# A feed-forward block in float32: both products by one step of a seven-product scheme, with the second weight matrix streamed from DRAM

## The chip, the cores and the metric

The kernel runs on one core of one Trainium2 chip. A core has TensorE (PE in the profile: matmuls; its weight loads are listed apart as PEld), VectorE (DVE), ScalarE (ACT), GpSimd (POOL), SyncE (SP, which here only issues DMAs) and 16 DMA engines. Tiles lie in SBUF, 128 partitions wide; matmul results go to PSUM, eight banks of 512 float32 values per partition. Each engine works through its own instructions in order and waits on semaphores for the others. The metric is the time of one execution on the device in microseconds (us), the median of several runs.

## The reference

Linear attention with a normalization, then a feed-forward block with squared ReLU. All arrays are float32, except that the two weight matrices arrive as float64.

```python
kv = np.einsum('bhsd,bhse->bhde', k, v)           # B=8, H=8, S=576, D=64
out = np.einsum('bhsd,bhde->bhse', q, kv)
rms = np.sqrt(np.mean(out * out, axis=-1, keepdims=True) + 1e-06)
x = out / rms * g_norm                            # then (B, H, S, D) -> (4608, 512)
h = x @ w_in                                      # 512 x 2048
r = np.maximum(h, 0.0)
y = (r * r) @ w_out                               # 2048 x 512
```

The two feed-forward products have 2 x 4608 x 512 x 2048 multiply-adds; the attention has far fewer.

## The kernel before

The 4608 tokens are worked off in nine strips of 512 (N_STRIP, four tiles of 128 tokens each). For each strip the attention must deliver `xt[s]`, the transposed features (128 partitions x 4 chunks of the model width x 512 tokens).

**Attention slices.** The attention is cut into small functions put into one list, `slices`: `transposed_query` and `key_value` for each of four pairs of heads of a batch, then `query` (four matmuls, square on ScalarE L226, reduction and Newton steps on VectorE L228 to L237, the scaled `x_n` L239) and `features` (four transposes L250, a scaled copy to `xt` on ScalarE L251). `key_value` also starts the loads of a later unit (`load_next`: ten DMAs on SP). `ready[s]` is the number of slices after which strip s has its features. `attend(n)` emits slices up to number n.

**Feed-forward.** `up(s, fc)` makes one chunk of 128 of the 2048 hidden features for the 512 tokens: four matmuls (K in four chunks) of 128 x 128 weights with 512 moving columns (L290), ReLU on ScalarE (L294), square on VectorE (L296). 16 such chunks stay in SBUF as `gt`. `down(s, i, part)` makes 128 tokens x 512 outputs: 16 matmuls in four parts (L307), then a copy to SBUF and a store. Results of both share four PSUM banks (`fpsum`).

**Order of the work.** The order is written out by hand (manual schedule): for each strip 16 `up` steps, then 16 `down` steps, and after every step `attend` emits the share of the next strip's slices that is due: by step i, (i + 1) / 29 of them. So the attention of strip s+1 lies between the matmuls of strip s.

**Weights.** Both matrices are to lie in SBUF as float32 for the whole run. They come as float64 words, and 32 pieces (16 of W_in, 16 of W_out, each 128 x 512 values, 512 KB) are converted by `convert`: two ScalarE operations (L142, L158), and on VectorE two TENSOR_SCALARs (L143, L148), a SCALAR_TENSOR_TENSOR (L153) and an integer add (L159). Three raw buffers; a piece's conversion issues the load of the piece three further on (L124). The conversions start before strip 0 and go on between its steps, three pieces for two steps, so that a piece of W_out is converted by the time `down` of strip 0 needs it.

Of the kernel before, what the change touches and what calls it, by code (L numbers as in the profile page):

```python
# [19 lines left out]
def kernel(  # L20
# [32 lines left out]
    N_TILE = n_tok // P  # L53
    NT = 4
    STRIP = NT * P
    N_STRIP = N_TILE // NT
# [3 lines left out]
    qkv_pool = ctx.enter_context(tc.tile_pool(name="qkv", bufs=3))  # L60
# [6 lines left out]
    raw_pool = ctx.enter_context(tc.tile_pool(name="raw", bufs=3))  # L67
    wtmp = ctx.enter_context(tc.tile_pool(name="wtmp", bufs=2))
    r_pool = ctx.enter_context(tc.tile_pool(name="r", bufs=2))
    g_pool = ctx.enter_context(tc.tile_pool(name="g", bufs=FC + 2))  # L70
    osb_pool = ctx.enter_context(tc.tile_pool(name="osb", bufs=2))
    apsum = ctx.enter_context(tc.tile_pool(name="apsum", bufs=4, space=bass.MemoryType.PSUM))
    fpsum = ctx.enter_context(tc.tile_pool(name="fpsum", bufs=4, space=bass.MemoryType.PSUM))
    ctx.enter_context(tc.manual_schedule())


# [25 lines left out]
    def load_next():  # L102
        u = next(to_load, None)
        if u is not None:
            load(*u)

    for _ in range(3):
# [6 lines left out]
    w_in_v = moe_w_in.rearrange("(kc p) (j f) -> j kc p f", p=P, f=WN)  # L114
    w_out_v = moe_w_out.rearrange("(fc p) e -> fc p e", p=P)
    pieces = [(w_in_v[j, kc], w_in[:, kc, ts(j, WN)]) for j in range(d_ff // WN) for kc in range(NP)]
    N_IN = len(pieces)
    pieces += [(w_out_v[fc], w_out[:, fc, :]) for fc in range(FC)]
    raw = []

    def load_piece():
        if len(raw) < len(pieces):
            t = raw_pool.tile([P, WN], I64, name="raw", tag="raw")
            nc.sync.dma_start(out=t, in_=pieces[len(raw)][0])  # L124
            raw.append(t)


    LEAST, MOST = 2.0**-15, float.fromhex("0x1.DFFFFEp+16")
    piece_at = [0]

    def convert(n):
        while piece_at[0] < min(n, len(pieces)):
            i = piece_at[0]
            words = raw[i].bitcast(I32).rearrange("p (n two) -> p n two", two=2)
            low = raw[i].bitcast(U32).rearrange("p (n two) -> p n two", two=2)[:, :, 0]
            high = words[:, :, 1]
            high_f = raw[i].bitcast(FP32).rearrange("p (n two) -> p n two", two=2)[:, :, 1]
            dest = pieces[i][1].bitcast(I32)


            c = wtmp.tile([P, WN], FP32, name="w_c", tag="w_c")
            nc.scalar.activation(c, high_f, AF.Abs)  # L142
            nc.vector.tensor_scalar(  # L143
                out=c, in0=c, scalar1=LEAST, scalar2=MOST, op0=ALU.max, op1=ALU.min
            )

            ci = c.bitcast(I32)
            nc.vector.tensor_scalar(  # L148
                out=ci, in0=ci, scalar1=3, scalar2=0x3FFFFFFF,
                op0=ALU.logical_shift_left, op1=ALU.bitwise_and,  # L150
            )

            nc.vector.scalar_tensor_tensor(  # L153
                out=dest, in0=high, scalar=-(2**30), in1=ci, op0=ALU.bitwise_and, op1=ALU.bitwise_or
            )

            r = wtmp.tile([P, WN], I32, name="w_r", tag="w_r")
            nc.scalar.activation(r, low, AF.Copy, scale=2.0**-29)  # L158
            nc.vector.tensor_tensor(out=dest, in0=dest, in1=r, op=ALU.add)  # L159
            load_piece()  # L160
            piece_at[0] += 1

    for _ in range(3):
        load_piece()
# [10 lines left out]
    qT, kvd, x_n, xt = {}, {}, {}, {}  # L175
# [67 lines left out]
    def features(n):  # L243
        s, i = divmod(n, NT)
        t = x_n.pop(n)
        if s not in xt:
            xt[s] = xt_pool.tile([P, NP, STRIP], FP32, name="xT", tag="xT")
        ps = apsum.tile([P, NP, P], FP32, name="xt_ps", tag="at")
        for p in range(NP):
            nc.tensor.transpose(ps[:, p, :], t[:, ts(p, P)], ident)  # L250
        nc.scalar.activation(xt[s][:, :, ts(i, P)], ps, AF.Copy, scale=g_col)  # L251

    slices, ready = [], {}
    for b in range(B):
        for p in range(NP):
            slices += [(transposed_query, (b, p)), (key_value, (b, p))]
        first = b // 2 * PAIR + (C if b % 2 else 0)
        ns = list(range(first, first + C + b % 2))
        for i, n in enumerate(ns + [None]):
            if n is not None:  # L260
                slices.append((query, (n,)))
            if i > 0:
                slices.append((features, (ns[i - 1],)))
                if ns[i - 1] % NT == NT - 1:
                    ready[ns[i - 1] // NT] = len(slices)
# [19 lines left out]
    gt = {}  # L285

    def up(s, fc):
        ps = fpsum.tile([P, STRIP], FP32, name="h_ps", tag="f")
        for kc in range(NP):
            nc.tensor.matmul(  # L290
                ps, lhsT=w_in[:, kc, ts(fc, P)], rhs=xt[s][:, kc, :], start=(kc == 0), stop=(kc == NP - 1)
            )
        r = r_pool.tile([P, STRIP], FP32, name="r", tag="r")
        nc.scalar.activation(r, ps, AF.Relu)  # L294
        t = g_pool.tile([P, STRIP], FP32, name="gt", tag="gt")
        nc.vector.tensor_tensor(out=t, in0=r, in1=r, op=ALU.mult)  # L296
        gt[fc] = t

    OQ = 4
    o_ps = [None]  # L300

    def down(s, i, part):
        if part == 0:
            o_ps[0] = fpsum.tile([P, d_model], FP32, name="o_ps", tag="f")
        n = FC // OQ
        for fc in range(part * n, (part + 1) * n):
            nc.tensor.matmul(  # L307
                o_ps[0], lhsT=gt[fc][:, ts(i, P)], rhs=w_out[:, fc, :], start=(fc == 0), stop=(fc == FC - 1)
            )
        if part == OQ - 1:  # L310
            o_sb = osb_pool.tile([P, d_model], FP32, name="o_sb", tag="o_sb")
            (nc.scalar.copy if i % 2 else nc.vector.tensor_copy)(o_sb, o_ps[0])  # L312
            for part_, rows in out_rows(NT * s + i):
                nc.sync.dma_start(out=rows, in_=o_sb[part_])

    for i in range(ready[0]):
        attend(i + 1)
        convert(i // 2 - 5)
    for s in range(N_STRIP):
        attend(ready[s])  # L320
        steps = [(up, (s, fc)) for fc in range(FC)]
        steps += [(down, (s, i, part)) for i in range(NT) for part in range(OQ)]
        goal = ready.get(s + 1, len(slices))
        for i, (fn, a) in enumerate(steps):
            if s == 0:

                convert(NP + 2 + 3 * i // 2)
            fn(*a)
            attend(ready[s] + (goal - ready[s]) * (i + 1) // (len(steps) - 3))


# [28 lines left out]
```

## Time and profile before

| | before |
|---|---|
| median of 3 runs | 1158.25 us (1158.03 to 1159.32) |
| the profiled execution, its own time | 1158.05 us |
| its span in the trace | 1156.2 us |
| granted TensorE clock, mean | 0.988 |
| TensorE busy | 1115.7 us (96%) |
| VectorE, ScalarE, GpSimd busy | 272.4, 210.7, 10.5 us |
| moved by DMA | 55.10 MB, 48 GB/s on average |

How to read the lines that follow. A line of the groups has: source line, engine, operation, output tile <- input tiles, shapes, count | busy us, mean ns of one instruction | idle us of its engine just before them and what ended it. The mean of a matmul is its latency from first to last element, with its way through the array; neighbours overlap, so the time that each adds is read from the distance between starts, or from the chain. A line of the chain of waits in order of time has: start, us, what was on the path, and of how many instructions. A line of the timeline has: start, us, engine, line, operation. A line of the windows has: window, its length, busy us and count of each engine, TensorE clock, share of the DMA engines, GB/s. A line of the DMA issues has: count, KB each, median us from issue to landing.

### The profile page before, as it was taken

To read this page: it belongs to the slowest core of one execution; us is meant where nothing else is said; L and a number is where in the kernel's file an instruction comes from. 1 tells how busy PE (TensorE), PEld (TensorE's weight loads), DVE (VectorE), ACT (ScalarE), POOL (GpSimd) and SP (SyncE) were. 2 spreads that over 40 slices of the span, in tenths; PEclk is the share of its full clock that TensorE was granted. 3 is DMA by queue.
4 is the path that set the end of the run, shared out by engine and by line. 5 is a ranking of instruction groups with operands and counts; after the bars stand their busy time and mean duration, and the time that the engine had idled before them with its cause. 6 is when DMAs were issued, how large, how long until landed. Compare 5 with 4: busy or idle time off the path is not lost.

```text
span 1156.2 us, 8506 instructions
## 1 busy us (share of the span) xinstructions
PE 1115.7 (96%) x3232; PEld 545.0 (47%) x3232; DVE 272.4 (24%) x590; ACT 210.7 (18%) x400; POOL 10.5 (1%) x70
## 2 busy tenths in 40 slices
PE   3699799999999999999999999999999999999998
PEld 3355354545445554454445444445445544444443
DVE  0789711212122122102111122102220122101200
ACT  1565311211121012101121112101220112001100
POOL 1000000000000000000000000000000000000000
PEclk8899899999999999999999999999999999999999
DMA  7567400220012100220012100230010000000000
GB/s 197 160 212 233 128 10 18 54 63 26 19 31 61 40 19 9 62 71 19 9 31 62 49 19 1 54 85 21 0 31 10 18 10 1 9 19 9 1 18 19
DMA packets 100169, 55.10 MB, mean 48 GB/s; under 512 B 83232, under 2 KB 91424, under 8 KB 100128
## 3 DMA queue, kind: packets, MB, share of 16 engines
q1 hardware_dynamic: 99968, 54.55, 17.0%
q8 instruction: 26, 0.43, 0.2%
q14 instruction: 15, 0.12, 0.0%
q10 hardware_dynamic: 160, 0.00, 0.0%
HBM read 45.09 MB, written 9.44 MB: 47 GB/s over the span
## 4 chain that ended last, share of the span: by engine, by line
PE 93%; SPq 2%; DVE 2%; DMA 1%; ACT 1%; issue 0%; DVEq 0%; ACTq 0%
PE h_ps L290 43%; PE o_ps L307 42%; PE kv_ps L197 2%; PE x_ps L223 2%; PE xt_ps L250 1%; PE t_ps L182 1%; SPq L91 1%; PE kv_ps L198 1%; SPq L95 1%; DMA raw<-in_moe_w_out_dram 0%; DMA q<-in_q_dram 0%; PE x_ps L218 0%; DVE w_c L148 0%; SPq L86 0%; DVE w_out L153 0%
## 5 line engine op out<-in xcount | busy, mean ns | idle before, releaser
L307 PE MATMUL o_ps<-w_out,gt 128*128 128x512 f32 x1152 | 513.0, 598 | 6.7 <-DVE w_out L159 6.7
L290 PE MATMUL h_ps<-xT,w_in 128*128 128x512 f32 x1152 | 508.3, 596 | 1.5 <-ACT xT L251 0.8
L290 PEld LDWEIGHTS h_ps<-xT,w_in 128*128 128x128 f32 x1152 | 215.4, 191 | 255.4 <-issue 248.2
L307 PEld LDWEIGHTS o_ps<-w_out,gt 128*128 128x128 f32 x1152 | 214.5, 191 | 255.4 <-issue 243.5
L296 DVE TENSOR_TENSOR gt<-r 128x512 f32<-128x512 f32 x144 | 99.6, 691 | 414.1 <-ACT r L294 414.1
L294 ACT ACTIVATE r<-h_ps 128x512 f32<-128x512 f32 x144 | 85.8, 596 | 365.5 <-PE h_ps L290 365.4
L228 DVE TENSOR_REDUCE ms<-sq 128x8 f32<-128x512 f32 x36 | 24.6, 684 | 157.3 <-ACT sq L226 157.3
L226 ACT ACTIVATE sq<-x_ps 128x512 f32<-128x512 f32 x36 | 21.4, 596 | 163.8 <-PE x_ps L223 140.1
L312 DVE COPY o_sb<-o_ps 128x512 f32<-128x512 f32 x18 | 12.5, 692 | 163.5 <-PE o_ps L307 163.4
L197 PEld LDWEIGHTS kv_ps<-v,k 128*128 128x128 f32 x256 | 35.9, 205 | 13.4 <-issue 13.4
L251 ACT ACTIVATE xT<-xt_ps,g_col 128x512 f32<-128x512 f32 x36 | 24.6, 683 | 93.2 <-PE xt_ps L250 93.2
L223 PEld LDWEIGHTS x_ps<-kvd,qT 128*128 128x128 f32 x256 | 33.6, 194 | 13.6 <-issue 13.6
L182 PE MATMUL t_ps<-ident,q 128*128 128x128 f32 x128 | 20.7, 288 | 18.6 <-DMA q<-in_q_dram 18.6
L197 PE MATMUL kv_ps<-v,k 128*128 128x128 f32 x256 | 36.3, 289 | 0.0
L223 PE MATMUL x_ps<-kvd,qT 128*128 128x128 f32 x256 | 34.1, 277 | 0.0
L312 ACT COPY o_sb<-o_ps 128x512 f32<-128x512 f32 x18 | 10.5, 586 | 123.8 <-PE o_ps L307 123.8
L182 PEld LDWEIGHTS t_ps<-ident,q 128*128 128x128 f32 x128 | 16.6, 148 | 33.9 <-issue 31.4
L250 PE MATMUL xt_ps<-ident,x_n 128*128 128x128 f32 x144 | 22.2, 278 | 9.7 <-DVE x_n L239 5.2
L250 PEld LDWEIGHTS xt_ps<-ident,x_n 128*128 128x128 f32 x144 | 18.0, 143 | 27.3 <-issue 16.2
L184 ACT COPY qT<-t_ps 128x512 f32<-128x512 f32 x32 | 18.6, 582 | 61.8 <-PE t_ps L182 61.8
L206 DVE COPY kvd<-kv_ps 64x64 f32<-64x64 f32 x32 | 7.3, 228 | 83.4 <-ACT kvd L205 83.2
L142 ACT ACTIVATE w_c<-raw 128x512 f32<-128x512 f32 x32 | 21.7, 678 | 28.3 <-DMA raw<-in_moe_w_out_dram 16.2
(32 smaller groups left out, 222.4 us busy)
## 6 DMA issues: line engine op xcount, KB each, us to landing
k<-in_k_dram SPq DMA_DIRECT2D x64, 128.0 KB, 3.0
v<-in_v_dram SPq DMA_DIRECT2D x32, 256.0 KB, 3.2
q<-in_q_dram SPq DMA_DIRECT2D x64, 128.0 KB, 3.0
raw<-in_moe_w_in_dram SPq DMA_DIRECT2D x16, 512.0 KB, 3.6
raw<-in_moe_w_out_dram SPq DMA_DIRECT2D x16, 512.0 KB, 3.7
out_dram<-o_sb SPq DMA_DIRECT2D x32, 256.0 KB, 2.3
k_rest<-in_k_dram SPq DMA_DIRECT2D x32, 32.0 KB, 2.9
v_rest<-in_v_dram SPq DMA_DIRECT2D x32, 32.0 KB, 2.7
```

The costliest lines, as they stand in the source:

```text
L142: nc.scalar.activation(c, high_f, AF.Abs)
L182: nc.tensor.transpose(ps[:, c, :], flat(t[:, c]), ident)
L197: nc.tensor.matmul(ps, lhsT=flat(tk[:, c]), rhs=tv[:, :, c, :], start=(c == 0), stop=False)
L223: nc.tensor.matmul(o, lhsT=qT[b, p][:, c_b, :], rhs=kvd[b, p], start=True, stop=True)
L228: nc.vector.reduce_sum(out=ms, in_=by_head(sq), axis=AX.X)
L250: nc.tensor.transpose(ps[:, p, :], t[:, ts(p, P)], ident)
L251: nc.scalar.activation(xt[s][:, :, ts(i, P)], ps, AF.Copy, scale=g_col)
L290: nc.tensor.matmul(ps, lhsT=w_in[:, kc, ts(fc, P)], rhs=xt[s][:, kc, :], start=(kc == 0), stop=(kc == NP - 1))
L294: nc.scalar.activation(r, ps, AF.Relu)
L296: nc.vector.tensor_tensor(out=t, in0=r, in1=r, op=ALU.mult)
L307: nc.tensor.matmul(o_ps[0], lhsT=gt[fc][:, ts(i, P)], rhs=w_out[:, fc, :], start=(fc == 0), stop=(fc == FC - 1))
L312: (nc.scalar.copy if i % 2 else nc.vector.tensor_copy)(o_sb, o_ps[0])
```

## The change

Both matrix products of a strip are done as 2 x 2 blocks by one step of Strassen's scheme in Winograd's form: seven block products instead of eight, with sums of blocks ahead of and behind them.

- **Blocks of `up`.** W_in is halved along the model width (KH = 2 chunks of 128) and along the hidden features (FH = 1024); the strip's features are halved along the model width and along the tokens (TH = 256). So a matmul in `up` now has 256 moving columns. `w_in` holds seven blocks: the four (one of them overwritten by a difference) and three sums.
- **Blocks of `down`.** The hidden values G are halved along the hidden features and the tokens, W_out along the hidden features and the outputs (DH = 256). Matmuls have 256 moving columns too.
- **Weights.** Pieces are the same size, but each has two runs of 256 columns. After four pieces of W_in, or two of W_out, GpSimd makes four sums or differences of 512 elements a partition (`sums_in`, `sums_out`). W_out's seven blocks don't stay in SBUF: after each two pieces they are written to a DRAM tensor of 7 MB (896 KB a time), and `stream` reads one block of 1 MB for each product of each `down`, three ahead, on SP. The pools of raw pieces and temporaries are closed after the conversions; the stream's three buffers and the output buffers take their space.
- **Order of conversions.** There are 44 items now (32 pieces, 12 groups of sums). Five are issued in each of the four groups of `up` of strip 0, a group ahead; what is left is issued in one block before `down` of strip 0.
- **Features.** `sums_x`, a new attention slice, makes four sums of the features on VectorE (512 elements each) once a strip's features are there.
- **Products.** A step `up(s, g, p)` is one block product for two feature chunks: 8 matmuls of 256 columns, into one bank. The order of products is 1, 2, 6, 5, 7, 3, 4. Products 6, 7 and 4 go on adding to the bank of product 1 (A), product 3 to that of product 5 (B); product 2 has bank C. In between, `combine` takes snapshots on ScalarE (after 1, 6 and 5) or adds bank and snapshot on VectorE (after 2, 7 and 3); product 4's bank is C21 itself. Bank A has two buffers, B and C one each.
- **After `up`.** ReLU and square are now a VectorE add out of PSUM and one VectorE instruction for three quarters, and two ScalarE instructions for the last. VectorE also makes G's sums: two in `up`, two long ones (2048 elements a partition) in `down`.
- **`down(s, p, i)`** is 8 matmuls of 256 columns, two such steps for each product; behind each product the next block's read is issued; each quarter of the output is stored in rows of 256 values.
- **Attention.** `qkv` has two buffers each instead of three. The share of slices due is now counted by weight (an `up` step 1, a `down` step 2, 56 in a strip) and reaches all of them at 85% of the strip (47.6).

```diff
-    w_in = wpool.tile([P, NP, d_ff], FP32, name="w_in")
-    w_out = wpool.tile([P, FC, d_model], FP32, name="w_out")
+    w_in = wpool.tile([P, 7, KH, FH], FP32, name="w_in")
+    w_out = dram.tile([7, P, FQ, DH], FP32, name="w_out")
...
+    def sums_in(g):
+        a11, a21, a12, a22, s1, s2, s4 = (w_in[:, b, :, ts(g, WN // 2)] for b in range(7))
+        nc.gpsimd.tensor_tensor(out=s1, in0=a21, in1=a22, op=ALU.add)
+        minus(nc.gpsimd, s2, s1, a11)
+        minus(nc.gpsimd, s4, a12, s2)
+        minus(nc.gpsimd, a21, a11, a21)
...
+    def sums_out(j):
+        b11, b12, b21, b22, t1, t2, t4 = (wt[j][:, b, :] for b in range(7))
+        minus(nc.gpsimd, t1, b12, b11)
+        minus(nc.gpsimd, t2, b22, t1)
+        minus(nc.gpsimd, b12, b22, b12)
+        minus(nc.gpsimd, t4, b21, t2)
+        nc.sync.dma_start(out=w_out[:, :, j, :].rearrange("b p e -> p b e"), in_=wt.pop(j))
...
+    def product(p, i, lhsT, rhs, n):
+        for k in range(n):
             nc.tensor.matmul(
-                ps, lhsT=w_in[:, kc, ts(fc, P)], rhs=xt[s][:, kc, :], start=(kc == 0), stop=(kc == NP - 1)
+                bank[BANK[p]][:, i, :], lhsT=lhsT(k), rhs=rhs(k),
+                start=p in (1, 5, 2) and i == 0 and k == 0, stop=k == n - 1, skip_group_check=True,
             )
...
+    def combine(p, c11, c12, c21, c22):
+        b = bank[BANK[p]]
+        if p in (1, 6, 5):
+            snap[p] = snap_pool.tile([P, 2, 2 * P], FP32, name=f"snap{p}", tag=f"snap{p}")
+            nc.scalar.copy(snap[p], b)
+        elif p == 4:
+            c21(b)
+        else:
+            other, c = {2: (1, c11), 7: (5, c22), 3: (6, c12)}[p]
+            c(b, snap[other])
...
+        def relu_squared(q):
+            def f(b, a):
+                o = dest[q]
+                nc.vector.tensor_tensor(out=o, in0=b, in1=a, op=ALU.add)
+                nc.vector.scalar_tensor_tensor(out=o, in0=o, scalar=0.0, in1=o, op0=ALU.max, op1=ALU.mult)
+                if q == 12:
+                    nc.vector.tensor_tensor(out=dest[1], in0=dest[12], in1=dest[22], op=ALU.add)
+                    minus(nc.vector, dest[12], dest[11], dest[12])
+            return f
...
+    def stream():
+        u = next(to_stream, None)
+        if u is not None:
+            w_blk[u] = stream_pool.tile([P, FQ, DH], FP32, name="w_blk", tag="w_blk")
+            nc.sync.dma_start(out=w_blk[u], in_=w_out[B_OUT[u[1]]])
...
+        steps = [(1, up, (s, g, p)) for g in range(NG) for p in ORDER]
+        n_up = len(steps)
+        steps += [(2, down, (s, p, i)) for p in ORDER for i in range(2)]
...
+            if s == 0 and i < n_up:
+                convert((NP + 1) * (a[1] + 1) + (i % len(ORDER)) * (NP + 1) // len(ORDER) + 1)
+            elif s == 0 and i == n_up:
+                convert(len(conversions))
+                conv.close()
+                stream_pool = ctx.enter_context(tc.tile_pool(name="stream", bufs=3, reuse_waits="tile"))
+                osb_pool = ctx.enter_context(tc.tile_pool(name="osb", bufs=3, reuse_waits="tile"))
+                for _ in range(3):
+                    stream()
             fn(*a)
-            attend(ready[s] + (goal - ready[s]) * (i + 1) // (len(steps) - 3))
+            done += w
+            attend(min(goal, ready[s] + int((goal - ready[s]) * done / (0.85 * total))))
```

More of the change, by code (lines that the diff above doesn't have):

```diff
@@ L105, in load_next @@
             load(*u)
-    for _ in range(3):
+    for _ in range(2):
         load_next()
-    w_in = wpool.tile([P, NP, d_ff], FP32, name="w_in")
-    w_out = wpool.tile([P, FC, d_model], FP32, name="w_out")
+    KH, FH, DH = NP // 2, d_ff // 2, d_model // 2
+    FQ = FC // 2
     WN = 512
-    w_in_v = moe_w_in.rearrange("(kc p) (j f) -> j kc p f", p=P, f=WN)
-    w_out_v = moe_w_out.rearrange("(fc p) e -> fc p e", p=P)
-    pieces = [(w_in_v[j, kc], w_in[:, kc, ts(j, WN)]) for j in range(d_ff // WN) for kc in range(NP)]
@@ L117 @@
-    N_IN = len(pieces)
-    pieces += [(w_out_v[fc], w_out[:, fc, :]) for fc in range(FC)]
+    NG = FQ // 2
+    w_in = wpool.tile([P, 7, KH, FH], FP32, name="w_in")
+    w_out = dram.tile([7, P, FQ, DH], FP32, name="w_out")
+    w_in_v = moe_w_in.rearrange("(kc p) (b g f) -> kc g p b f", p=P, b=2, g=NG)
+    w_out_v = moe_w_out.rearrange("(fc p) (b e) -> fc p b e", p=P, b=2)
+    wt = {}
+    sources = [w_in_v[kc, g] for g in range(NG) for kc in range(NP)]
+    sources += [w_out_v[j + b * FQ] for j in range(FQ) for b in range(2)]
@@ L119 @@
     raw = []
     def load_piece():
-        if len(raw) < len(pieces):
-            t = raw_pool.tile([P, WN], I64, name="raw", tag="raw")
-            nc.sync.dma_start(out=t, in_=pieces[len(raw)][0])
+        if len(raw) < len(sources):
+            t = raw_pool.tile([P, 2, WN // 2], I64, name="raw", tag="raw")
+            nc.sync.dma_start(out=t, in_=sources[len(raw)])
             raw.append(t)
     LEAST, MOST = 2.0**-15, float.fromhex("0x1.DFFFFEp+16")
-    piece_at = [0]
-    def convert(n):
[L132 to L161, printed above, removed]
@@ new lines, in convert_piece @@
+    def convert_piece(i, dest):
+        view = lambda dt: raw[i].bitcast(dt).rearrange("p b (n two) -> p b n two", two=2)
+        low, high, high_f = view(U32)[:, :, :, 0], view(I32)[:, :, :, 1], view(FP32)[:, :, :, 1]
+        c = wtmp.tile([P, 2, WN // 2], FP32, name="w_c", tag="w_c")
+        nc.scalar.activation(c, high_f, AF.Abs)
+        nc.vector.tensor_scalar(out=c, in0=c, scalar1=LEAST, scalar2=MOST, op0=ALU.max, op1=ALU.min)
+        ci = c.bitcast(I32)
+        nc.vector.tensor_scalar(
+            out=ci, in0=ci, scalar1=3, scalar2=0x3FFFFFFF,
+            op0=ALU.logical_shift_left, op1=ALU.bitwise_and,
+        )
+        dest = dest.bitcast(I32)
+        nc.vector.scalar_tensor_tensor(
+            out=dest, in0=high, scalar=-(2**30), in1=ci, op0=ALU.bitwise_and, op1=ALU.bitwise_or
+        )
+        r = wtmp.tile([P, 2, WN // 2], I32, name="w_r", tag="w_r")
+        nc.scalar.activation(r, low, AF.Copy, scale=2.0**-29)
+        nc.vector.tensor_tensor(out=dest, in0=dest, in1=r, op=ALU.add)
+        load_piece()
@@ new lines, in minus, with piece_in @@
+    def minus(eng, out, a, b):
+        eng.tensor_tensor(out=out, in0=a, in1=b, op=ALU.subtract)
+    def piece_in(i):
+        g, kc = divmod(i, NP)
+        b = kc // KH * 2
+        convert_piece(i, w_in[:, b : b + 2, kc % KH, ts(g, WN // 2)])
+    def sums_in(g):
[4 more added lines that the diff above has]
+        minus(nc.gpsimd, a21, a11, a21)
@@ L163 @@
+    conversions = []
+    for g in range(NG):
+        conversions += [(piece_in, NP * g + kc) for kc in range(NP)] + [(sums_in, g)]
+    for j in range(FQ):
+        conversions += [(piece_out, 2 * j), (piece_out, 2 * j + 1), (sums_out, j)]
+    converted = [0]
+    def convert(n):
+        while converted[0] < min(n, len(conversions)):
+            fn, a = conversions[converted[0]]
+            fn(a)
+            converted[0] += 1
     for _ in range(3):
@@ L251, in features, with sums_x @@
         nc.scalar.activation(xt[s][:, :, ts(i, P)], ps, AF.Copy, scale=g_col)
+    xc = {}
+    def sums_x(s):
+        x = lambda kh, th: xt[s][:, kh * KH : (kh + 1) * KH, ts(th, TH)]
+        xc[s] = t1, t2, t3, t4 = [
+            xc_pool.tile([P, KH, TH], FP32, name=f"x_t{i}", tag=f"x_t{i}") for i in range(4)
+        ]
+        minus(nc.vector, t1, x(0, 1), x(0, 0))
+        minus(nc.vector, t2, x(1, 1), t1)
+        minus(nc.vector, t3, x(1, 1), x(0, 1))
+        minus(nc.vector, t4, x(1, 0), t2)
     slices, ready = [], {}
@@ L264 @@
                 if ns[i - 1] % NT == NT - 1:
+                    slices.append((sums_x, (ns[i - 1] // NT,)))
                     ready[ns[i - 1] // NT] = len(slices)
@@ L282, in out_rows, with open_bank @@
         return [(slice(0, P), out[b * S : b * S + C * P, :].rearrange("(sp c) e -> c sp e", c=C)[c_b])]
[L285 to L289, printed above, removed]
+    ORDER = (1, 2, 6, 5, 7, 3, 4)
+    BANK = {1: "A", 6: "A", 7: "A", 4: "A", 5: "B", 3: "B", 2: "C"}
+    A_IN = {1: 0, 2: 2, 3: 6, 4: 3, 5: 4, 6: 5, 7: 1}
+    B_OUT = {1: 0, 2: 2, 3: 3, 4: 6, 5: 4, 6: 5, 7: 1}
+    bank, snap, gq, w_blk = {}, {}, {}, {}
+    def open_bank(p):
+        b = BANK[p]
+        if p in (1, 5, 2):
+            bank[b] = fpsum.tile([P, 2, 2 * P], FP32, name=f"ps_{b}", tag=b, bufs=2 if b == "A" else 1)
+        return bank[b]
@@ L302, in down @@
[L302 to L314, printed above, removed]
+                bank[BANK[p]][:, i, :], lhsT=lhsT(k), rhs=rhs(k),
@@ new lines, with down, store, f @@
+    to_stream = iter([(s, p) for s in range(N_STRIP) for p in ORDER])
+    def stream():
[3 more added lines that the diff above has]
+            nc.sync.dma_start(out=w_blk[u], in_=w_out[B_OUT[u[1]]])
+    def down(s, p, i):
+        if i == 0:
+            open_bank(p)
+        a = gq[s, {1: 11, 2: 21, 6: 11, 5: 1, 7: 12, 3: 21, 4: 22}[p]]
+        w = w_blk[s, p]
+        product(p, i, lambda fc: a[:, fc, ts(i, P)], lambda fc: w[:, fc, :], FQ)
+        if i == 0:
+            return
+        del w_blk[s, p]
+        stream()
+        if p == 1:
+            minus(nc.vector, gq[s, 11], gq[s, 1], gq[s, 11])
+        if p == 2:
+            minus(nc.vector, gq[s, 21], gq[s, 21], gq[s, 11])
+        def store(th, eh):
+            def f(b, a=None):
+                o = osb_pool.tile([P, 2, DH], FP32, name="o_sb", tag="o_sb")
+                if a is None:
+                    nc.scalar.copy(o, b)
+                else:
+                    nc.vector.tensor_tensor(out=o, in0=b, in1=a, op=ALU.add)
+                for t in range(2):
+                    for part, rows in out_rows(NT * s + 2 * th + t):
+                        nc.sync.dma_start(out=rows[:, ts(eh, DH)], in_=o[part, t, :])
+            return f
+        combine(p, store(0, 0), store(0, 1), store(1, 0), store(1, 1))
```

55 lines of the change are left out of this document (36 added, 19 removed).

## The prediction

> **What bounds the kernel now.** I read the page first, its list of engines and its chain of work that ended last.
>
> ```profile
> span 1156.2 us, 8506 instructions
> PE 1115.7 (96%) x3232; PEld 545.0 (47%) x3232; DVE 272.4 (24%) x590; ACT 210.7 (18%) x400; POOL 10.5 (1%) x70
> PE 93%; SPq 2%; DVE 2%; DMA 1%; ACT 1%; issue 0%; DVEq 0%; ACTq 0%
> ```
>
> TensorE is both the busiest engine and 93% of the path. Next, the chain in order of time, which gives exact durations of uninterrupted runs of passes.
>
> ```profile
> 53.93 4.56 PE h_ps L290 x10
> 139.03 7.18 PE o_ps L307 x10
> 153.96 0.44 PE xt_ps L250 x4
> 157.84 0.89 PE x_ps L223 x8
> 1042.36 54.93 PE h_ps L290 x128
> 1097.30 54.95 PE o_ps L307 x128
> ```
>
> The last strip has no attention work beside it: 128 passes of `up` and 128 of `down` back to back, 429.3 ns for a pass of 512 columns (54.95 / 128). The groups of instructions by line say how many there are.
>
> ```profile
> L307 PE MATMUL o_ps<-w_out,gt 128*128 128x512 f32 x1152 | 513.0, 598 | 6.7 <-DVE w_out L159 6.7
> L290 PE MATMUL h_ps<-xT,w_in 128*128 128x512 f32 x1152 | 508.3, 596 | 1.5 <-ACT xT L251 0.8 <-DVE w_in L159 0.8
> ```
>
> The kernel writes 9 x 64 matmuls for each product and the trace has 1152 passes: every float32 matmul is two passes. So 2304 x 0.4293 = 989 us of the span are feed-forward passes, and almost none of them waits. The one place where something else is late is strip 0. The timeline of VectorE there:
>
> ```profile
> 48.19 0.69 DVE L159 CUSTOM_DVE_ANT_0 w_in<-w_in,w_r 128x1024 uint16<-128x1024 uint16 x1
> ...
> 129.15 0.42 DVE L143 TENSOR_SCALAR w_c<-w_c 128x512 f32<-128x512 f32 x1
> 129.60 0.43 DVE L148 TENSOR_SCALAR w_c<-w_c 128x512 int32<-128x512 int32 x1
> 130.07 0.69 DVE L153 SCALAR_TENSOR_TENSOR w_out<-raw,w_c 128x512 int32<-128x512 int32 x1
> 130.89 0.69 DVE L159 CUSTOM_DVE_ANT_0 w_out<-w_out,w_r 128x1024 uint16<-128x1024 uint16 x1
> 131.50 0.42 DVE L143 TENSOR_SCALAR w_c<-w_c 128x512 f32<-128x512 f32 x1
> ...
> 138.28 0.69 DVE L159 CUSTOM_DVE_ANT_0 w_out<-w_out,w_r 128x1024 uint16<-128x1024 uint16 x1
> ```
>
> A weight piece costs VectorE 2.35 us (129.15 to 131.50), a 512-element operation 0.61 us from start to start (130.89 to 131.50). The last conversion that `down` of strip 0 needs ends at 138.97, and `down` runs freely from 139.03: TensorE waited for the conversions.
>
> **Fewer passes.** Seven products of 8 x 2 matmuls (N = 256) in `up` and as many in `down`: 112 + 112 matmuls, 448 passes a strip, 4032 in all, where there were 2304 of 512. No row has 256 columns. From below: half of 429.3, 214.7 ns. From above: the x_ps row has passes of 128 columns at 111 ns (0.89 / 8); a line through 111 and 429.3 gives 217.3. Each of those short passes has its own weight load, so twice as many loads per column hide there already, too. I take 216, the middle: 4032 x 0.216 = 871 us, 118 less than 989 (113 to 123 by the ends). One strip is 96.8 us instead of 109.9.
>
> From 139.03 on the old kernel does `down` of strip 0 (54.95), eight whole strips (8 x 109.88 = 879.0), and 1156.2 - 139.03 - 55.0 - 879.0 = 83.2 us of attention, clock ramp (10 passes take 7.18 instead of 4.29 at 139.03) and the final store. The attention is untouched and as far along at that point (the code asks for 28/47.6 = 59% of the next strip's slices after `up`, it asked for 16/29 = 55%), so the 83.2 stay. Call T the moment when `down` of strip 0 starts. The new span is T + 48.4 + 774.1 + 83.2 = T + 905.7, plus new stalls.
>
> **T: conversions, sums and the DRAM round trip.** All 32 pieces must now be converted, summed on GpSimd, written out and read back before the first `down` product. Twenty-five of 44 conversion items are issued by the end of `up`; the other 19 (12 pieces, seven sums) come in one block with no TensorE work between them. VectorE is at 48.9 when three pieces are done; then `sums_x` of strip 0 (4 x 0.61 = 2.4), so 51.3. In the old kernel the rest up to 138.97 held 29 pieces (68.2), 16 squares (9.8) and 9.6 us of attention and waits. Now: 68.2 + 9.6 and, for four groups, eight operations each (sums out of PSUM, relu-squared, G sums): 32 x 0.61 = 19.5. That is 97.3: the last piece would be done at 148.6. TensorE has 224 passes of `up` (48.4 us) and a few slices to do in this time and waits for the rest; that wait is inside T and is not counted again.
>
> GpSimd gets 48 operations of 512 elements with two inputs. The rows of its engine that are nearest:
>
> ```profile
> masks.py:199 POOL TENSOR_SCALAR_AFFINE_SELECT ident<-ident 128x128 f32<-128x128 f32 x1 | 0.3, 292 | 0.1
> L344 POOL MEMSET const-float32-0.0<- 128x1 f32 x1 | 0.1, 104 | 0.2 <-issue 0.2
> ```
>
> (292 - 104) / 128 is 1.47 ns an element for one input: 104 + 512 x 1.47 = 0.86 us; with two inputs read in turn up to 1.61. I take 1.2: 57.6 us for all 48. The Trainium skill, GPSIMD Engine Reference, Performance versus the Vector engine, has 4497 ns for a two-input float32 add of 2048 elements; a quarter of it, an estimate of 1.12 us, would make the sum 54 us.
>
> Does GpSimd work beside VectorE? Where the two met in strip 0, the timeline has:
>
> ```profile
> 115.72 0.43 DVE L143 TENSOR_SCALAR w_c<-w_c 128x512 f32<-128x512 f32 x1
> 116.18 0.43 DVE L148 TENSOR_SCALAR w_c<-w_c 128x512 int32<-128x512 int32 x1
> 116.64 0.69 DVE L153 SCALAR_TENSOR_TENSOR w_out<-raw,w_c 128x512 int32<-128x512 int32 x1
> ```
> ```profile
> 115.62 0.14 POOL L203 MEMSET kvd<- 64x64 f32 x1
> 115.81 0.43 POOL L204 MEMSET kvd<- 64x64 f32 x1
> 116.29 0.41 POOL L203 MEMSET kvd<- 64x64 f32 x1
> 116.73 0.15 POOL L204 MEMSET kvd<- 64x64 f32 x1
> ```
>
> A memset of 0.14 us took 0.43 and 0.41 when it began inside a TENSOR_SCALAR, and ended with it: it was held for the whole operation. Beside the SCALAR_TENSOR_TENSOR it was not held, but a memset reads nothing. The new operations read two operands, and so do L153 and L159. Cheap end: only the two TENSOR_SCALARs of a piece exclude GpSimd, and the 57.6 us hide but for their last four. Dear end: all four do, and the work of both engines adds up. I take the dear end, since the only meeting in which both engines had something to share ended in a full block. The Trainium skill, SBUF — State Buffer, Who interferes with whom, says that a VectorE instruction with two SBUF inputs contends with a GpSimd instruction that reads SBUF, not with one that only writes; the held and unheld memsets agree with it as far as they go, and by this rule the dear end holds.
>
> Dear end: 97.3 + 57.6, less what can overlap (12 sums with one input in PSUM, 7.3; half of the 9.6, 5): 142.6, so GpSimd ends at 193.9. Then a write of 896 KB and a read of 1 MB, one after the other.
>
> ```profile
> raw<-in_moe_w_out_dram SPq DMA_DIRECT2D x16, 512.0 KB, 3.7
> out_dram<-o_sb SPq DMA_DIRECT2D x32, 256.0 KB, 2.3
> 18.00:24.00 6.00, 3.29 (x14) 2.91 (x14) 0.23 (x1) 0.79 (x2) 0.00 (x0) 0.72 1.01 319
> ```
>
> From 2.3 us for 256 KB and 3.7 for 512: 5.6 us a MB on a base of 0.9, so 5.8 and 6.5, 12.3 in all; at the 319 GB/s of the window from 18 to 24 us (its last column) on the same base 8.0. I take 10. T = 204.
>
> **Handovers in PSUM.** Every group has four places where TensorE adds to a bank that ScalarE or VectorE must read first (products 6, 7, 3 and 4), each with one product between them.
>
> ```profile
> L294 ACT ACTIVATE r<-h_ps 128x512 f32<-128x512 f32 x144 | 85.8, 596 | 365.5 <-PE h_ps L290 365.4
> L296 DVE TENSOR_TENSOR gt<-r 128x512 f32<-128x512 f32 x144 | 99.6, 691 | 414.1 <-ACT r L294 414.1
> ```
>
> The cover is 8 passes, 1.73 us. A pass ends some 0.17 after its stream (598 - 429 ns), the read takes 0.60 to 0.69: some 0.85 us is spare. A query slice's chain (square, reduction, root, Newton steps) can hold ScalarE's or VectorE's queue longer. Its places are few (four queries a strip): half a microsecond a strip, 4 us. If the cover were gone, 144 handovers would cost 0.8 us each. In `down` the product between lasts 6.9 us; the long G subtractions (four times 0.69 at most) lie there.
>
> **The stream.** 63 blocks of 1 MB, three read ahead, one used up in 2 x 16 x 0.216 = 6.9 us. At 6.5 us a block they keep pace, and three blocks lie ready when `down` begins; in the queue of SP they pass stores and loads of 0.6 us to issue. I cost them, the half-wide stores, the thinner query buffers and `sums_x` (2.4 us a strip on a VectorE that is 24% busy) at nothing; what hides them is 96.8 us of TensorE a strip.
>
> **Sum.** 204 + 905.7 + 4 = 1113.7 us of span; the profiled execution took 1158.05 with a span of 1156.2, so 1.85 more: 1115.6, and its own time is within 0.2 us of the median of 1158.25. I say 1116. The ends: GpSimd's operation 0.86 to 1.61 us (-16, +20), the pass (-5, +5), the round trip (-2, +2), handovers up to +10: 1092 to 1142.
>
> **Rivals.** *GpSimd works beside VectorE* (the cheap end). Last piece at 148.6; in the last block SP's write of one pair waits for its sums and the loads wait behind it: write 0.6, load 0.3 + 3.7, conversion 3.0, sums 4.8 are 12.4 for two pairs where VectorE needs 9.4, 9 us more over six; last sums 4.8, round trip 10: T = 172, time 1084 (1066 to 1095). For it: the unheld memset. Against: that memset read nothing.
>
> *Handovers bite.* At 0.2 us over the cover, 144 x 0.2 = 29: 1145. For it: ScalarE and VectorE serve attention in the same queues. Against: 0.85 us spare.
>
> *Slower: half-wide passes do not take half the time.* The change doubles the weight loads per column. If 12 ns more of each stayed uncovered, 4032 x 0.012 = 48 us: 1164. It decides from 226.5 ns a pass on ((1158.25 - 1116) / 4032 = 10.5 more). Then the change does not do what it says. Against it: 111 ns a pass at 128 columns, in runs of eight, loads included; nothing in the trace shows a long run of such passes.
>
> **How the numbers follow.** Forecast 0.60, GpSimd beside VectorE 0.24, handovers 0.10, slow passes 0.06. The range 1070 to 1142 leaves out the lowest eighth of the second (0.03), a tail of the first (0.03), two thirds of the third (0.07) and the last (0.06). The measurement tells 0.2% (2.3 us) from no change: faster 0.92, same 0.02 (handovers that eat all), slower 0.06.
>
> **What would show it.** Passes of 256 columns 216 ns apart; 4032 of them; GpSimd and VectorE operations stretched in strip 0; a TensorE gap of some 70 us that ends near 204; no waits of `down` for the streamed blocks; under 10 us of TensorE waiting for ScalarE or VectorE after strip 0. The forecast is wrong if the gap ends near 172, or if the strips after it take over 108 us of feed-forward time.

## The result and the profile after

The changed kernel takes 1126.86 us (median of 4 runs, 1125.41 to 1129.28) where the kernel before took 1158.14 in the same comparison: a ratio of 0.9732, with a 95% interval of 0.9712 to 0.9751. The forecast was 1116, with a range of 1070 to 1142. The profiled execution took 1126.69 us with a span of 1124.9.

The first lines of the page of the changed kernel, with the span, the busy time of each engine and, by slices of 28 us, TensorE's busy time and granted clock:

```profile
span 1124.9 us, 12527 instructions
PE 1003.8 (89%) x4960; PEld 878.9 (78%) x4960; DVE 461.5 (41%) x797; ACT 243.9 (22%) x454; POOL 61.2 (5%) x118
...
PE   3456920699999999999999999999999999999998
...
PEclk9888965799999999999999999999999999999999
```

TensorE is busy 112 us less than before, but the span is only 31 us shorter. The first eight digits, 3 4 5 6 9 2 0 6, say where: TensorE is busy for 90 of the first 200 us, and from some 206 us on it is full.

The chain of waits in order of time, around the start of `down` of strip 0 and in the last strip:

```profile
197.48 4.05 DMA w_out<-wt
201.65 4.77 DMA w_blk<-w_out
206.55 5.27 PE ps_A L364 x16
...
1079.48 6.91 PE ps_C L364 x32
```

`down` of strip 0 starts at T = 206.55, after the last write of W_out's blocks and the read of the first one. In the last strip 32 passes take 6.91 us: a pass of 256 columns is 215.9 ns. The first 16 passes at T take 5.27 us instead of 3.46; the granted clock of the slices before and around T is 0.5 and 0.7.

The timeline of TensorE in the second group of `up`:

```profile
78.23 1.99 PE L364 MATMUL ps_A<-x_t,w_in 128*128 128x256 f32 x8 [1.14 <-DVE w_in L170]
80.06 0.59 PE L364 MATMUL ps_A<-xT,w_in 128*128 128x256 f32 x2
86.99 2.93 PE L364 MATMUL ps_A<-xT,w_in 128*128 128x256 f32 x6 [6.34 <-DVE w_in L170]
...
111.83 0.80 PE L364 MATMUL ps_A<-xT,w_in 128*128 128x256 f32 x1 [4.20 <-DVE w_in L170]
```

A step of `up` is four matmuls of the code, so eight passes (The change counts these as eight matmuls). Product 1 of the group does its first two passes at 80.06 and then waits for a conversion until 86.99. From one such place to the next it is 24.8 us (86.99 to 111.83), though a group's passes take 12.1. The conversion that it waits for is issued just ahead of product 1 and belongs to the *next* group of columns, which product 1 doesn't use. (The view ends at 112 us, so its last line counts one of the six passes that start at 111.83.) The waits, TensorE's alone:

```profile
PE ps_A L364 <- DMA w_blk<-w_out: 58.4, 1, 58.4
PE ps_A L364 <- DVE w_in L170: 29.9, 6, 14.1
...
PE ps_B L364 <- ACT snap L374: 1.2, 1, 1.2
...
PE ps_A L364 <- DVE gt L399: 0.6, 1, 0.6
```

The last two lines are all that TensorE waited for handovers in PSUM in the whole run, 1.8 us. No line names a streamed block but the first read at T: the stream keeps pace.

### The profile page after: what moved, and what is told of

It is laid out like the page before. It is cut to its first block, busy times and chain, and to the rows that moved or that the text cites. A ratio compares the mean times of both kernels' runs of the same rounds, so it can differ in the third digit from the quotient of the medians.

```text
span 1124.9 us, 12527 instructions
## 1 busy us (share of the span) xinstructions
PE 1003.8 (89%) x4960; PEld 878.9 (78%) x4960; DVE 461.5 (41%) x797; ACT 243.9 (22%) x454; POOL 61.2 (5%) x118
## 4 chain that ended last, share of the span: by engine, by line
PE 84%; DVE 9%; DMA 3%; SPq 1%; POOL 1%; issue 1%; ACT 1%; DVEq 0%; POOLq 0%; ACTq 0%
PE ps_A L364 43%; PE ps_B L364 21%; PE ps_C L364 11%; PE x_ps L275 2%; PE kv_ps L249 2%; PE xt_ps L302 1%; PE t_ps L234 1%; PE kv_ps L250 1%; DMA raw<-in_moe_w_out_dram 1%; DVE w_c L155 1%; DVE w_c L158 1%; DVE w_in L170 1%; DVE gt L400 1%; DVE w_in L164 1%; DVE wt L164 1%
## 5 line engine op out<-in xcount | busy, mean ns | idle before, releaser
L364 PE MATMUL ps_A<-w_blk,gt 128*128 128x256 f32 x1152 | 259.1, 381 | 58.4 <-DMA w_blk<-w_out 58.4
L364 PEld LDWEIGHTS ps_A<-w_blk,gt 128*128 128x128 f32 x1152 | 218.0, 191 | 88.1 <-issue 58.8
L364 PE MATMUL ps_A<-x_t,w_in 128*128 128x256 f32 x864 | 206.6, 382 | 6.0 <-DVE w_in L170 5.3
L364 PEld LDWEIGHTS ps_A<-x_t,w_in 128*128 128x128 f32 x864 | 161.8, 190 | 29.7 <-DVE w_in L170 6.3
L364 PE MATMUL ps_B<-w_blk,gt 128*128 128x256 f32 x576 | 128.5, 379 | 0.0
L364 PEld LDWEIGHTS ps_B<-w_blk,gt 128*128 128x128 f32 x576 | 108.4, 190 | 14.3 <-issue 0.2
L174 DVE TENSOR_TENSOR gt<-gt 128x512 f32<-128x512 f32 (+1 forms) x54 | 69.0, 1279 | 87.4 <-PE ps_A L364 57.7
L364 PE MATMUL ps_A<-xT,w_in 128*128 128x256 f32 x288 | 74.1, 401 | 24.6 <-DVE w_in L170 24.6
L399 DVE TENSOR_TENSOR gt<-ps_C,snap 128x512 f32<-128x512 f32 x36 | 24.9, 692 | 160.1 <-PE ps_C L364 160.1
L400 DVE SCALAR_TENSOR_TENSOR gt<-gt 128x512 f32<-128x512 f32 x108 | 76.7, 710 | 3.7
L364 PE MATMUL ps_C<-xT,w_in 128*128 128x256 f32 x288 | 69.9, 386 | 0.0
L399 DVE TENSOR_TENSOR gt<-ps_A,snap 128x512 f32<-128x512 f32 x36 | 24.9, 691 | 105.2 <-PE ps_A L364 104.7
```

What stands on the lines that cost most here:

```text
L174: eng.tensor_tensor(out=out, in0=a, in1=b, op=ALU.subtract)
L364: nc.tensor.matmul(bank[BANK[p]][:, i, :], lhsT=lhsT(k), rhs=rhs(k), start=p in (1, 5, 2) and i == 0 and k == 0, stop=k == n - 1, skip_gro ...
L399: nc.vector.tensor_tensor(out=o, in0=b, in1=a, op=ALU.add)
L400: nc.vector.scalar_tensor_tensor(out=o, in0=o, scalar=0.0, in1=o, op0=ALU.max, op1=ALU.mult)
```

## The experiments

My theory after the two traces: the passes went as reckoned, what lies behind T nearly so, and what eats the gain is TensorE's idle time ahead of T. It has three parts: the false wait above, VectorE's work with GpSimd taking turns with it, and the round trip through DRAM. The rivals: VectorE is busy anyway and the false wait only shows where TensorE queues; the order of SyncE's queue; the DMA engines.

**W_in in four tiles.** The second chunk of K in product 1 lies, in the one W_in tile, between the first and the last address of that conversion's two strided blocks.

```diff
-    w_in = wpool.tile([P, 7, KH, FH], FP32, name="w_in")
+    w_in = [wpool.tile([P, 7, KH, WN // 2], FP32, name=f"w_in{g}") for g in range(NG)]
```

> The converted W_in blocks lie in four tiles, one for each group of up, instead of one tile; nothing else changes. Theory A (a false wait: in the changed kernel the second K chunk of product 1 of group g waits for the first piece of group g+1, because that piece's destination spans its addresses; TensorE and VectorE then take turns in a group): the groups of up shrink from 24.5 us to the some 19 us of VectorE's own work with GpSimd's share, T falls from 206.6 by 15 to 30 us, time 1097 to 1112 us. Theory B (VectorE with GpSimd is busy all the time and sets T; the wait only shows where TensorE queues): T moves by less than 4 us, time 1123 to 1128 us.

Measured: 1108.01 us (1105.52 to 1108.95), a ratio of 0.9574 (0.9557 to 0.9591). The chain of waits in order of time:

```profile
178.64 4.05 DMA w_out<-wt
...
187.76 5.62 PE ps_A L364 x16
```

and the timeline of TensorE:

```profile
71.42 1.89 PE L364 MATMUL ps_A<-xT,w_in 128*128 128x256 f32 x8
...
87.92 2.49 PE L364 MATMUL ps_A<-x_t,w_in 128*128 128x256 f32 x8 [3.93 <-DVE gt L399]
...
91.27 2.60 PE L364 MATMUL ps_A<-xT,w_in 128*128 128x256 f32 x8
```

Product 1 runs its eight passes in one go, the group takes 19.9 us (71.42 to 91.27), T is 187.76, 18.8 earlier. Theory A holds. What TensorE waits for now is a sum out of PSUM (L399) that stands in VectorE's queue behind conversions.

**The same by addresses alone.** One tile, the group outermost: `w_in = wpool.tile([P, NG, 7, KH, WN // 2], ...)`, with the indices to match.

> W_in's blocks stay in one tile, but the group of up is its outermost dimension, so that the addresses of a group are contiguous; nothing else changes. Theory A (the false wait comes from the span of addresses of a piece's strided destination, which covers blocks of the group before): the gain of the four tiles is had again, T within 2 us of 187.8, time 1104 to 1111 us. Theory B (the wait comes from sharing one tile): T stays at 206.6, time 1124 to 1129 us.

Measured: 1108.14 us (1106.52 to 1108.79), T = 187.72. The tile is still shared and the wait is gone, so it came from the span of addresses of a strided destination, not from the shared tile.

**The writes on GpSimd's queue.** In the block of conversions ahead of `down` VectorE converts two pieces of W_out, a pair, in 6.45 us ((182.32 - 156.52) / 4; the expectations say 6.4). Its timeline in the changed kernel, and how long it waited there for a buffer of `wt` (in the view of the waits):

```profile
156.52 0.42 DVE L155 TENSOR_SCALAR w_c<-w_c 128x512 f32<-128x512 f32 x1
...
182.32 0.42 DVE L155 TENSOR_SCALAR w_c<-w_c 128x512 f32<-128x512 f32 x1
```
```profile
DVE wt L164 <- DMA w_out<-wt: 1.0, 2, 0.5
...
DVE wt L164 <- POOL wt L174: 0.6, 1, 0.6
```

The edit:

```diff
-        nc.sync.dma_start(out=w_out[:, :, j, :].rearrange("b p e -> p b e"), in_=wt.pop(j))
+        nc.gpsimd.dma_start(out=w_out[:, :, j, :].rearrange("b p e -> p b e"), in_=wt.pop(j))
```

> The writes of W_out's sums to DRAM are issued from GpSimd's queue, behind the sums themselves, so that the raw loads on SyncE's queue no longer stand behind a write that waits. Theory A (the order on SyncE's queue sets the 6.4 us of a pair in the block ahead of down): the pair falls to 5.5 us or less, T falls by 5 us or more, time 1121 us or less. Theory B (the DMA engines are full there, 1.97 MB a pair at 305 GB/s, or VectorE with GpSimd's share is): the pair stays within 0.3 us of 6.4, time 1124 to 1129 us.

Measured: 1130.33 us (1127.97 to 1131.41), a ratio of 0.9768 (0.9751 to 0.9785), T = 208.7. No gain, a loss of some 2 us: just outside what theory B gave, and on the other side of theory A. The pair takes 6.9 us, also more than theory B gave. The loads now wait for no write, and nothing is gained: the order of SyncE's queue does not set the pace. What is new is that VectorE waits 5.7 us in all for writes of a buffer that it needs, where it waited 1.0. A write is issued in 0.97 us on GpSimd (the groups by line of this run), where SyncE needs 0.38 (the instructions of `wt` in the changed kernel), and lands after 5.8 us instead of 4.9:

```profile
L200 POOL DMA_DIRECT2D w_out<-wt x8 | 7.8, 972 | 2.4 <-POOL wt L174 2.1 <-DMA w_out<-wt 0.3
```
```profile
L200 SPq DMA_DIRECT2D w_out<-wt x8: 377/377/387, 144.1 to 197.5; - x8
```

**The two engines side by side, measured by themselves.** In the kernel before, in strip 7, four GpSimd subtractions of two operands or six memsets, and six VectorE adds of two SBUF operands or six TENSOR_SCALARs, alone and beside each other, on scratch tiles.

> The kernel before, with groups of operations on scratch tiles added in strip 7, where VectorE is mostly idle: four GpSimd subtractions alone (512 and 256 elements), six VectorE adds of two SBUF operands or six TENSOR_SCALARs alone, and both side by side; also GpSimd memsets beside each. The output is not touched. Theory A (exclusive): four subtractions of 512 beside six adds take about the sum of both, 7.5 us or more, single operations stretch by up to the length of one of the other engine; memsets beside adds do not stretch, memsets beside TENSOR_SCALARs do. Theory B (only TENSOR_SCALARs exclude GpSimd): subtractions beside adds end in about the longer of the two, 5.2 us, without stretching.

The timeline, GpSimd (subtractions of 512 alone, of 256 alone, 512 beside adds, 256 beside adds, 512 beside TENSOR_SCALARs, memsets beside adds, memsets beside TENSOR_SCALARs):

```profile
941.41 5.63 POOL L324 TENSOR_TENSOR probec<-probea,probeb 128x512 f32<-128x512 f32 x4 [237.12 <-DVE probec L341]
948.74 3.47 POOL L324 TENSOR_TENSOR probec<-probea,probeb 128x256 f32<-128x256 f32 x4 [1.71 <-DVE probec L341]
969.31 6.54 POOL L324 TENSOR_TENSOR probec<-probea,probeb 128x512 f32<-128x512 f32 x4 [17.10 <-DVE probec L341]
983.93 4.44 POOL L324 TENSOR_TENSOR probec<-probea,probeb 128x256 f32<-128x256 f32 x4 [8.08 <-DVE probec L341]
991.47 5.48 POOL L324 TENSOR_TENSOR probec<-probea,probeb 128x512 f32<-128x512 f32 x4 [3.10 <-DVE probec L341]
1007.85 3.45 POOL L336 MEMSET probec<- 128x512 f32 x6 [10.90 <-DVE probec L341]
1013.11 4.39 POOL L336 MEMSET probec<- 128x512 f32 x6 [1.81 <-DVE probec L341]
```

and VectorE (adds alone, TENSOR_SCALARs alone, adds beside 512, adds beside 256, TENSOR_SCALARs beside 512, adds beside memsets, TENSOR_SCALARs beside memsets):

```profile
954.91 4.26 DVE L328 TENSOR_TENSOR probef<-probed,probee 128x512 f32<-128x512 f32 x6
...
961.77 2.67 DVE L332 TENSOR_SCALAR probef<-probed 128x512 f32<-128x512 f32 x6
...
969.08 8.04 DVE L328 TENSOR_TENSOR probef<-probed,probee 128x512 f32<-128x512 f32 x6
983.77 5.88 DVE L328 TENSOR_TENSOR probef<-probed,probee 128x512 f32<-128x512 f32 x6
991.25 6.45 DVE L332 TENSOR_SCALAR probef<-probed 128x512 f32<-128x512 f32 x6
1007.71 4.26 DVE L328 TENSOR_TENSOR probef<-probed,probee 128x512 f32<-128x512 f32 x6
1012.97 4.07 DVE L332 TENSOR_SCALAR probef<-probed 128x512 f32<-128x512 f32 x6
```

Six adds take 4.26 us alone and 8.04 beside four subtractions of 512: each subtraction takes 0.95 us from VectorE, one of 256 elements 0.40 ((5.88 - 4.26) / 4). Beside memsets the adds keep their 4.26. TENSOR_SCALARs lose 0.95 us to a subtraction of 512 too ((6.45 - 2.67) / 4), and 1.40 us to six memsets. So two-operand work on both engines excludes each other, theory A; but a subtraction costs VectorE less than it lasts. The runs of four "alone" were not quite alone, since squares of the kernel (L296, two SBUF operands) fell into them: one took 1.65 us instead of 0.69. A subtraction that met none took 1.27 us at 512 elements and 0.72 at 256, so the hold is about three quarters of it at 512 and a little over half at 256. The Trainium skill, SBUF — State Buffer, Who interferes with whom, has both halves of this, the adds that contend with GpSimd's reads and not with its writes, and the rows agree. Of VectorE's 2-port modes it also says that whoever comes first blocks the other for the whole instruction; which mode an operation ran in no run here shows, and no hold measured here is as long as the subtraction.

**All sums on VectorE.** `nc.gpsimd` becomes `nc.vector` in `sums_in` and `sums_out`.

> All 48 sums of weight blocks run on VectorE instead of GpSimd. Theory A (the two engines exclude each other while GpSimd reads: the sums cost VectorE nearly their time either way): VectorE gets 48 operations, some 16 x 0.61 + 32 x 0.35 = 21 us, and loses its stretching of 13 us and the waits for GpSimd; T within 8 us of 206.6, time 1119 to 1135 us. Theory B (GpSimd works beside VectorE, its sums are nearly free): T rises by the 21 us, time 1143 us or more.

Measured: 1122.28 us (1120.15 to 1123.23), a ratio of 0.9698 (0.9678 to 0.9717), T = 201.1. VectorE does 48 operations more and the kernel is no slower, it is a little faster. With the probe's prices GpSimd's sums took 16 x 0.95 + 32 x 0.40 = 28.0 us from VectorE; a timeline of the next kernel gives 1.47 us for four sums of 256 there, so its own sums take 16 x 0.61 + 32 x 0.37 = 21.6: 6.4 less, and T fell by 5.5. In the block a pair now takes 6.17 us, which is 4.70 for two pieces and 1.47 for four sums, and VectorE waits for nothing there: VectorE sets the pace, not the transfers.

**Both together.** Four tiles and the sums on VectorE.

> Both changes together: W_in's blocks in four tiles and all sums of weight blocks on VectorE. Theory A (two separate causes, the false wait worth 19 us and GpSimd's hold on VectorE worth 28 us against 21 us of its own work, that add): T some 6 us under the 187.8 of the four tiles alone, time 1099 to 1104 us. Theory B (with the false wait gone GpSimd works in gaps of VectorE, so that taking its work over costs): time 1112 us or more.

Measured: 1106.01 us, the median of runs of 1105.61, 1105.61, 1106.40 and 6022.35; what held up the last is not known, and the ratio of 0.9549 (0.9532 to 0.9567) leaves it out. T = 184.83, 2.9 ahead of the four tiles alone. Between the two expectations, nearer to A: T moved by 21.7 where the two alone moved it by 18.8 and 5.5, so the two prices do not quite add. That with the false wait gone part of GpSimd's hold falls into gaps of VectorE would explain it, but no run shows it.

**Two operations less a piece.** The changed kernel without the two TENSOR_SCALARs of a conversion (its weights are therefore not the converted ones).

> The changed kernel with the two TENSOR_SCALARs of each piece left out, so that the weights are not converted properly; all transfers stay. VectorE's work for a pair falls from 6.3 us to 4.6. Theory A (VectorE with GpSimd's hold sets the 6.4 us of a pair in the block ahead of down): the pair falls to 5.2 us or less. Theory B (the DMA engines set it, 1.97 MB at 305 to 333 GB/s): the pair stays at 5.9 us or more.

Measured: 1111.11 us (two runs, 1110.28 and 1111.94), T = 189.9. The timeline of VectorE, every fourth start of the block ahead of `down`:

```profile
151.76 0.69 DVE L159 SCALAR_TENSOR_TENSOR wt<-raw,w_c 128x512 int32<-128x512 int32 x1 [4.71 <-DMA w_out<-wt]
...
163.14 0.92 DVE L159 SCALAR_TENSOR_TENSOR wt<-raw,w_c 128x512 int32<-128x512 int32 x1 [1.85 <-DMA w_out<-wt]
...
174.83 0.69 DVE L159 SCALAR_TENSOR_TENSOR wt<-raw,w_c 128x512 int32<-128x512 int32 x1 [2.25 <-POOL wt L169]
```

A pair now takes 5.77 us ((174.83 - 151.76) / 4), between the two expectations, and VectorE waits in it for writes of the buffer that it needs. So VectorE with GpSimd's hold set the 6.4 us (4.70 + 4 x 0.40 = 6.3), and the transfers stand some 0.6 us behind: the DMA engines are full there (a share of 0.92 to 1.04 between 150 and 175 us), so making VectorE faster in the block gains little. Whether more than two buffers for `wt` would help was not tried by itself. Most of the 16.7 us by which T fell comes from ahead of the block, whose first conversion starts 13.6 us earlier (142.96, not 156.52).

**Work for TensorE in the gap.** From these results a version in which strip 0 needs no DRAM. `down` of strip 0 is done in plain form, chunk by chunk as W_out's pieces are converted; their sums, on GpSimd, run behind it for strip 1. W_in lies in four tiles, its sums are on VectorE, `wt` has three buffers (two scratch tiles have one buffer each to make room).

```diff
+    def down_plain(j):
+        convert(NG * (NP + 1) + 2 * (j + 1))
...
+        for t in range(NT):
+            th, i = divmod(t, 2)
+            for fh in range(2):
+                nc.tensor.matmul(
+                    acc[t].rearrange("p b e -> p (b e)"),
+                    lhsT=gq[0, ((11, 12), (21, 22))[fh][th]][:, j, ts(i, P)],
+                    rhs=w[:, 2 * fh * DH : 2 * (fh + 1) * DH],
+                    start=j == 0 and fh == 0, stop=j == FQ - 1 and fh == 1,
+                )
+        sums_out(j)
+        convert(NG * (NP + 1) + 2 * min(j + 4, FQ))
```

> Four tiles and W_in's sums on VectorE; besides, down of strip 0 is done in plain eight-product form with 512 columns, chunk by chunk as W_out's pieces are converted (no sums of G in strip 0); the sums of W_out run behind it and serve from strip 1 on. Theory A (what eats the gain is TensorE's idle time ahead of down of strip 0): TensorE gets 55 us of work in that time, the round trip through DRAM lies behind up of strip 1, strip 0 ends near 192 us and the time is 1055 to 1075 us. Theory B (the chain of a chunk, product, sums, write, next conversion into the same buffer, sets a longer period of 9 us or more): 1080 to 1100 us.

Measured: 1063.19 us (1062.18 to 1063.86), a ratio of 0.9181 (0.9163 to 0.9199). At the end of strip 0 TensorE still waited for a bank, whose copy waited for the first store:

```profile
189.46 1.89 PE L364 MATMUL ps_A<-xT,w_in 128*128 128x256 f32 x8
195.89 3.78 PE L364 MATMUL ps_C<-xT,w_in 128*128 128x256 f32 x8 [4.54 <-ACT o_sb L443]
```

**Four output buffers, laid first.** `bufs=4` for the output pool, opened ahead of the stream's.

> The version with the plain down of strip 0 (1063 us), with four output buffers instead of three, laid ahead of the stream's buffers, so that the four copies of strip 0 need not wait for the last weight writes or the first store (TensorE waited 4.5 us for a bank there). Theory A (that wait is on the path): 1056 to 1060 us. Theory B (the wait for the streamed blocks or for VectorE takes its place): 1061 to 1064 us.

Measured: 1057.40 us (1056.85 to 1058.86), a ratio of 0.9132 (0.9116 to 0.9147): theory A. It is the fastest version here. The timeline at the same place:

```profile
191.51 1.89 PE L364 MATMUL ps_A<-xT,w_in 128*128 128x256 f32 x8
193.23 1.89 PE L364 MATMUL ps_C<-xT,w_in 128*128 128x256 f32 x8
```

## Why the prediction was right, and where its sum was off

*The pass* of 256 columns: 216 ns predicted, 215.9 measured, in runs of 32 and more. The slower rival falls: twice as many weight loads stay covered.

*The whole.* The span was to be 1113.7 us and is 1124.9: 2.5 of the difference lies ahead of T and 8.7 behind it. The time is in the range and the mechanism held, but one term behind T was too small, and ahead of T two errors nearly cancelled.

*What follows T.* Predicted 905.7 + 4, measured 1124.9 - 206.55 = 918.4. The failing term is the 83.2 us of attention, ramp and tail that I took over from the old kernel. I took all 128 passes of its strip 0 `down` to come after 139.03. The groups of the old kernel in the window from 139 us on show otherwise:

```profile
L307 PE MATMUL o_ps<-w_out,gt 128*128 128x512 f32 x1122 | 498.0, 596 | 3.0 <-DVE w_out L159 3.0
```

1122 of 1152: 30 passes, 12.9 us, were already done, between conversions. The term is 83.2 + 12.9 = 96.1. The changed kernel has 3808 passes after T, 822.1 us, and 96.2 of other time. So this old strip 0 was better than the forecast held it to be, and the changed one loses by that much more. The 4 us for handovers, of which 1.8 came, hid a part of it.

*Handovers.* 4 us predicted, 1.8 in the waits of the whole run. That rival falls.

*T.* 204 predicted, 206.55 measured, but two steps of it were wrong and cancelled, which was luck. I added 57.6 us of GpSimd to VectorE's 97.3 and took 12.3 back: 45.3. The sums of W_out have 256 elements a partition, not the 512 that I misread (in The change too), and a subtraction holds VectorE for less than it lasts: an estimate of 28.0 by the probe's prices, if each meets work of VectorE. The 18.8 us of the false wait were not in the sum at all; the trace of the old kernel could not show it, since no conversion there had a destination of two strided blocks. 28.0 + 18.8 = 46.8. A slip of some 2.4 us comes on top: the 9.6 us of attention and waits were counted from 51.3, behind `sums_x`, which the old kernel doesn't have; from 48.9 to 138.97 they are 12.1. The gap of TensorE that ends at T is 58.4 us, not some 70. The upper ends as listed (20, 5, 2, and 10 of handovers where the sum has 4) add up to 1149 us, not 1142; the measured time lies below both. The direction that I took from one held memset, that two-operand work excludes each other, was borne out by the probe and by the sums on VectorE; the rival in which GpSimd works beside VectorE falls.

*The round trip* was 9.1 us (197.45, the end of the sums, to 206.55), 10 predicted.

The account of the whole: 2304 passes of 429.3 ns became 4032 of 215.9, 118.6 us less. TensorE's time ahead of T not spent on feed-forward passes was 139.03 - 158 x 0.4293 = 71.2 us and is 206.55 - 224 x 0.2159 = 158.2, 87.0 more. The difference, 31.6, is what the span shows (31.3). Nearly three quarters of the gain went back into the first 200 us. The last version had 69.5 of the 87.0 back (1126.86 to 1057.40): 18.9 of that is what the four tiles alone gave, and the rest came with W_in's sums on VectorE, the third buffer, `down` of strip 0 in plain form as work for TensorE in the gap, and the output buffers. These were not measured one by one, but for the last, 5.8.

Open: the sums on VectorE and the four tiles show the prices of the sums and of the false wait, T from one profiled execution each; how the rest of VectorE's time ahead of T splits between its own work and waits for TensorE was not taken apart.

## What to carry to other kernels

An algorithm with fewer multiplications saves what its passes cost, and that can be read off a trace before it is built; its price is paid where the operands are made, so look there for the engine that is late and for work that can stand in the gap. Before a term is carried over from an old trace, count which instructions lie on which side of the cut. In this kernel a destination of two strided blocks made TensorE wait for all that lies between them, 18.8 us in all: put the dimension by which work is staged outermost, or in tiles of its own, and look in the trace for a wait on data that isn't used.

## What the runs showed of the hardware

A GpSimd subtraction of two float32 operands kept VectorE's two-operand adds out for 0.95 us at 512 elements and 0.40 at 256, of its own 1.27 and 0.72, and TENSOR_SCALARs for 0.95 at 512 (256 was not tried). Six memsets cost six TENSOR_SCALARs 1.40 us and six two-operand adds nothing. TensorE passes of 256 columns, each with its own 128 x 128 weights, ran at 215.9 ns for some 900 us with a granted clock of 0.99 to 1.00. The issue of an 896 KB write took 0.97 us of GpSimd's queue and 0.38 of SyncE's.
